# Attention and squared-ReLU layers on one core: norm sums, token scales and the planner's engine choice rewritten

## The chip, the cores and the metric

The kernel runs on one core of one Trainium2 chip. The metric is the device time of one execution in microseconds. Three runs of the kernel before gave 688.0, 686.88 and 683.96 us; their median, 686.88 us, is the time that the change is compared with.

## What is computed

```python
def _attn_ref(q, k, v):                       # 4 batches, 12 heads, 448 tokens, 64 columns
    scores = (1 / sqrt(64)) * q @ k^T         # causal mask, softmax over the last axis
    return attn @ v
def _moe_ref(x, w_in, w_out):                 # x: 1792 tokens x 768; w_in 768 x 2048; w_out 2048 x 768
    r = np.maximum(x @ w_in, 0.0)
    return (r * r) @ w_out
```

The attention output of a batch, with its heads side by side, is the x of the second part. Everything comes in and goes out as float32.

## The kernel before, in words

Matrix products that need more than half precision are made of float16 pieces: a number is split into a high half (the helper `hi`, line 406) and the rest (the helper `lo`, line 419), and three products, high by high, high by rest and rest by high, are summed in PSUM. So that the halves stay in range, tensors are first scaled by powers of two that come from sums of squares (the helper `pow2`, line 436).

Attention works on pairs of heads, 24 pairs in all, six for each batch (`pair`, line 595). Batch 0 is done in float32 (scores on L677, transposes of the probabilities on L706, values on L718), batches 2 and 3 with float16 halves throughout (scores on L663, values on L728), batch 1 with float32 scores and float16 values. VectorE masks the scores and finds the row's extreme (L646), ScalarE takes the exponential (L650). Where values are float16, the normalised probabilities are split into halves in a tile psrc (`halves`, line 580), which a transposing DMA turns (L592). `pair_norm` (line 543) sums the squares of q and k for batches 2 and 3: ScalarE sums along rows (L548), one float32 matmul against a matrix of ones sums over partitions (L552).

The weights are loaded in 24 tiles of w_in and 16 of w_out, narrowed to float32 by integer operations (`narrow`, line 790), measured by Gram matrices on TensorE (L837, L878), and split into halves. In `weights_in` the largest entry of each of four groups is found through a diagonal tile dg (L847), which before is a buffer of the ring of the squares (`n_sq`, line 355), and a matmul with ones (L851).

The second part works on eight sub-blocks of 256 or 128 tokens (`sub_block`, line 928), two for each batch. Each has a head: ScalarE squares x of its six pairs (L938), six matmuls with ones add them over pairs and partitions (L943), three small VectorE operations make a power of two for each token (L950 to L956), three VectorE multiplications rescale x with it (L962), and `tau` (L967) makes the inverse scale on one partition; for each 128 tokens a matmul with one contracted row turns it to lie along partitions (L980), VectorE copies it out (L983) and forms the output factor (L985). Then come 16 blocks of 18 matmuls with w_in (L996), ReLU, square and split of each, and blocks of 6 matmuls with w_out (L1032). The first block of L996 in the program needs the x of all six pairs of batch 0, rescaled, and the first quarter of w_in's halves; the Gram matrices of w_out stand ahead of it in TensorE's queue.

All instructions are collected in a `Plan` (line 68) and put in order by its method `order` (line 149): it runs through a model of the engines, and at each step issues on some engine the ready operation with the smallest due time. Due times come from a table of numbers `PR` (line 21) by phase and kind of operation. Operations that several engines can do (halves, ReLU, copies and so on) carry a cost for each engine plus a bias from the same table; the planner passes over such an operation on an engine if another engine would end it sooner:

```python
if any(max(free.get(o, 0.0), cand[o][i]) + opts[o] + extra[o] < mine - 1e-9
       for o in opts if o != e): continue
```

The engines then execute their queues strictly in this order.

Of the kernel before, what the change touches and what calls it, by code (L numbers as in the profile page):

```python
# [7 lines left out]
F32 = mybir.dt.float32  # L8
# [13 lines left out]
    "bias_dve": 2396, "bias_act": -5582, "bias_pool": 2108, "T0": -417806, "RAMP": 114330, "B1": -987389,  # L22
# [7 lines left out]
    "m_fac": -4151640, "m_ghi": 2453041, "m_glo": -2429258, "m_msq": 1161753, "m_ob": 5245791, "m_relu": -3597239,  # L30
    "m_sig": 2979051, "m_sq": -2069264, "m_tau": 62051, "wi_wl": 127247, "wi_wn": 103676, "wi_wq": 2844441,
    "wo_wl": 2520234, "wo_wn": -2027194, "wo_wq": -1031725, "ws_wn": 2804128, "wt_wn": -555275,
    "a0_P.copy@act": -1188, "a0_P.copy@dve": -2443, "a0_P.nrm@act": -3840, "a0_P.nrm@dve": 4543,
    "a0_P.nrm@pool": 1096, "a0_qk.copy@act": 1118, "a0_qk.copy@dve": -3194, "a0_x.top@act": -2065,
    "a0_x.top@dve": -1734, "m_ghi.hi@act": -3891, "m_ghi.hi@dve": 3617, "m_ghi.hi@pool": -536, "m_glo.lo@dve": 5701,
    "m_glo.lo@pool": 4841, "m_relu.@act": -4348, "m_relu.@dve": -3168, "m_sq.@act": 3841, "m_sq.@dve": -2095,
# [31 lines left out]
class Plan:  # L68
# [80 lines left out]
    def order(self):  # L149
# [32 lines left out]
        while done < n:  # L182
            best = None
            for strict in (True, False):
                for e, c in cand.items():
                    if not c:
                        continue
# [7 lines left out]
                    if best is not None and t >= best[0]:  # L195
                        continue
# [932 lines left out]
```

## Time and profile before

| what | value |
|---|---|
| runs of the kernel | 688.0, 686.88, 683.96 us; median 686.88 us |
| span of the profiled execution, first to last instruction | 683.7 us |
| TensorE matmul busy | 632.0 us, 92% |
| VectorE, ScalarE, GpSimd busy | 349.6, 436.8, 225.2 us |
| mean granted TensorE clock | 0.967 |

The page gives the span of its execution and no device time of that execution beside it; the span lies 3.2 us under the median of the three runs and just under the fastest. A busy share is an average over a first stretch in which weights are prepared and a long one that is mostly matmuls, so the table alone does not say what bounds the time; the rows below are read by stretch. Busy times count overlapping instructions of one engine once, the mean duration of a group does not.

### The profile page before, as it was taken

Reading aid. Unit: us, or ns where it says so; the run is one execution under the profiler, and the core shown is the slowest. Engines: PE = TensorE matmul, PEld = TensorE weight load, DVE = VectorE, ACT = ScalarE, POOL = GpSimd, SP = SyncE. Lnnn points to the kernel's source line nnn. Section 1 sums busy time; section 2 is a strip of 40 time slices with the busy share of each in tenths; the row PEclk is TensorE's granted clock in tenths of the full one; section 3 lists DMA queues with packets and bytes.
Section 4 is the critical chain, followed back from the end, with each engine's and each line's share of the span. In section 5 each row is a group of like instructions: output and inputs, shape, how many; then the busy total and the mean of one; then the engine's idle time right before and its main releaser. Section 6 shows DMA issues by size and latency. Waiting matters only on the chain.

```text
span 683.7 us, 13868 instructions
## 1 busy us (share of the span) xinstructions
PE 632.0 (92%) x5110; PEld 457.6 (67%) x5110; DVE 349.6 (51%) x1027; ACT 436.8 (64%) x1260; POOL 225.2 (33%) x330
## 2 busy tenths in 40 slices
PE   5877779699999999999999999999999999999997
PEld 3554446476667676778675687768867878867864
DVE  3899898989986668788964543520100200200000
ACT  2688887879987997789667975754604434304500
POOL 4333233234521113344234864772302222103200
PEclk9987777989999999999999999999999999999999
DMA  9989886656476889999989936662000000000000
GB/s 263 293 246 283 276 308 220 152 133 121 89 128 132 176 166 177 190 173 177 198 159 184 206 70 102 122 135 43 13 23 13 13 13 1 13 23 12 13 23 24
DMA packets 208676, 87.31 MB, mean 128 GB/s; under 512 B 196064, under 2 KB 203488, under 8 KB 208608
## 3 DMA queue, kind: packets, MB, share of 16 engines
q1 hardware_dynamic: 208608, 86.43, 55.7%
q8 instruction: 40, 0.66, 0.4%
q14 instruction: 28, 0.23, 0.1%
HBM read 45.81 MB, written 5.51 MB: 75 GB/s over the span
## 4 chain that ended last, share of the span: by engine, by line
PE 46%; POOL 3%; DMA 3%; issue 3%; ACT 3%; DVE 2%; SPq 0%; DVEq 0%; POOLq 0%; ACTq 0%
PE bank L996 21%; PE bank L1032 21%; PE bank L728 2%; PE bank L663 1%; POOL psrc L431 1%; DMA raw<-in_k_dram 1%; POOL p L429 1%; DMA pT<-psrc 1%; ACT p L650 1%; DMA kT<-qs 1%; DVE psrc L426 1%; POOL g L421 1%; DVE bank L646 1%; ACT qs L413 0%; PE bank L980 0%
## 5 line engine op out<-in xcount | busy, mean ns | idle before, releaser
L996 PE MATMUL bank<-xt,wi 128*128 128x256 f16 (+1 forms) x2304 | 230.8, 259 | 1.3 <-ACT r L1007 1.2
L1032 PE MATMUL bank<-wo,g 128*128 128x384 f16 x1344 | 230.0, 326 | 0.0
L996 PEld LDWEIGHTS <-wi 128*128 128x128 f16 x2304 | 201.2, 98 | 25.4 <-issue 3.3
L1032 PEld LDWEIGHTS <-g 128*128 128x128 f16 x1344 | 129.4, 98 | 82.8 <-issue 2.9
L421 POOL TENSOR_TENSOR g<-g,g 128x256 f16<-128x256 f32 (+1 forms) x128 | 83.5, 663 | 232.0 <-ACT g L413 139.1
L650 ACT ACTIVATE p<-bank,nm 112x112 f32<-112x112 f32 (+3 forms) x192 | 93.3, 491 | 31.7 <-DVE nm L646 23.6
L1007 ACT ACTIVATE r<-bank 128x256 f32<-128x256 f32 (+1 forms) x128 | 45.4, 355 | 46.5 <-PE bank L996 45.9
L646 DVE CUSTOM_DVE_ANT_0 bank<-bank,mask,sc 112x336 f32<-112x336 f32 (+3 forms) x96 | 47.6, 512 | 51.1 <-PE bank L663 34.3
L1042 ACT ACTIVATE ob<-bank,fac 128x384 f32<-128x384 f32 x28 | 16.1, 578 | 82.4 <-PE bank L1032 82.3
L950 DVE TENSOR_SCALAR u<-bank 128x256 int32<-128x256 int32 (+1 forms) x8 | 3.1, 388 | 107.4 <-PE bank L943 45.7
L1014 ACT ACTIVATE g<-r 128x256 f32<-128x256 f32 (+1 forms) x128 | 48.8, 388 | 13.2 <-POOL g L421 9.6
L413 ACT ACTIVATE psrc<-p,nm 112x112 f16<-112x112 f32 (+2 forms) x106 | 49.7, 530 | 11.2 <-DMA pT<-psrc 8.1
L413 ACT ACTIVATE g<-g 128x256 f16<-128x256 f32 (+1 forms) x128 | 48.1, 389 | 12.9 <-PE bank L1032 11.4
L426 DVE SCALAR_TENSOR_TENSOR psrc<-p,nm,psrc 112x112 f16<-112x112 f32 (+3 forms) x96 | 52.6, 586 | 4.1 <-POOL psrc L415 2.2
L646 DVE CUSTOM_DVE_ANT_0 bank<-bank,mask 112x112 f32<-112x112 f32 (+3 forms) x96 | 41.1, 475 | 17.2 <-PE bank L677 16.9
L677 PE MATMUL bank<-kT,qT 64*112 64x336 f32 (+3 forms) x192 | 40.9, 471 | 6.7 <-ACT p L650 5.8
L706 PE MATMUL bank<-ident,p 112*112 112x112 f32 x120 | 28.9, 382 | 17.9 <-ACT p L566 14.0
L663 PE MATMUL bank<-kT,qT 128*112 128x336 f16 (+3 forms) x192 | 36.0, 286 | 3.4 <-ACT p L650 2.5
L650 ACT ACTIVATION_READ_ACCUMULATOR p<-bank,nm 112x1 f32 x192 | 38.5, 200 | 0.0
L706 PEld LDWEIGHTS bank<-ident,p 112*112 112x112 f32 x120 | 18.1, 187 | 28.8 <-ACT p L566 21.8
L431 POOL TENSOR_TENSOR psrc<-p,psrc 112x112 f16<-112x112 f32 (+3 forms) x48 | 35.0, 729 | 4.0
L728 PE MATMUL bank<-pT,vp 112*64 112x224 f16 (+3 forms) x432 | 31.2, 284 | 4.0 <-DMA pT<-psrc 4.0
(123 smaller groups left out, 747.3 us busy)
## 6 DMA issues: line engine op xcount, KB each, us to landing
raw<-in_moe_w_out_dram SPq DMA_DIRECT2D x8, 768.0 KB, 4.8
xt<-in_moe_w_out_dram SPq DMA_DIRECT2D x8, 768.0 KB, 5.2
xt<-in_moe_w_in_dram SPq DMA_DIRECT2D x11, 512.0 KB, 5.5
out_dram<-ob SPq DMA_DIRECT2D x28, 192.0 KB, 2.0
raw<-in_moe_w_in_dram SPq DMA_DIRECT2D x9, 512.0 KB, 6.5
vn<-in_v_dram SPq DMA_DIRECT2D x18, 224.0 KB, 3.0
raw<-in_v_dram SPq DMA_DIRECT2D x18, 224.0 KB, 3.5
raw<-in_q_dram SPq DMA_DIRECT2D x12, 224.0 KB, 3.4
```

The lines of the kernel that those rows point to most:

```text
L413: nc.scalar.activation(out=o, in_=i, func=ACTF.Copy, scale=s)
L421: return plan.add({"dve": dve_ns(n), "pool": pool2_ns(n)}, lambda e: engines[e].tensor_tensor(out=out(), in0=in_(), in1=top(), op=ALU.subt ...
L426: nc.vector.scalar_tensor_tensor(out=out(), in0=in_(), scalar=scale(), in1=top(), op0=ALU.mult, op1=ALU.subtract)
L646: one("dve", dve_ns(w, 1, 2 if F16S[b] else 1) - 10, lambda e: nc.vector.tensor_tensor_reduce(out=s.ap[0:P, 0:w], in0=s.ap[0:P, 0:w], in1= ...
L650: one("act", act_ns(w, True, 1, True), lambda e: nc.scalar.activation(out=p32[j].ap[:, b0:b0 + c + 1, :].rearrange("p a t -> p (a t)"), in ...
L663: nc.tensor.matmul(out=s.ap[0:P, 0:(c + 1) * P], lhsT=qT.ap[:, j * NCH + c, :], rhs=kT.ap[:, a:a + c + 1, :].rearrange("p a t -> p (a t)") ...
L706: nc.tensor.transpose(t.ap[0:P, (x - a) * P:(x - a + 1) * P], p32[j].ap[:, c * (c + 1) // 2 + kc, :], ident[0:P, 0:P])
L728: nc.tensor.matmul(out=pv.ap[j * D:(j + 1) * D, kc * P:S], lhsT=vp.ap[:, hv, vb:vb + D], rhs=pT[j].ap[0:P, hp * NSL + x:hp * NSL + x + w, ...
L996: nc.tensor.matmul(out=h.ap[:, 0:n], lhsT=wi_hl(ci, hw)[:, ms], rhs=x[:, kd, hx, off:off + n], start=(kd == 0 and hw == 0 and hx == 0), st ...
L1007: nc.scalar.activation(out=r.ap[:, 0:n], in_=h.ap[:, 0:n], func=ACTF.Relu)
L1014: nc.scalar.activation(out=g32.ap[:, 0:n], in_=r.ap[:, 0:n], func=ACTF.Square)
L1032: nc.tensor.matmul(out=o.ap[:, 0:HALF], lhsT=g[:, kf, hg, tt * 128:(tt + 1) * 128], rhs=wo_hl(kf, hw)[:, hh * HALF:(hh + 1) * HALF], start ...
```

## The change

These are its five parts.

1. The six squares of a sub-block lie side by side in one tile `sq`; three VectorE additions in bfloat16 (three pairs, one, one) sum them, and one matmul with ones takes the place of six.
2. The inverse token scale is made on all 128 partitions (it was on one). A VectorE multiplication with the identity matrix that also sums along the row puts it along partitions, in place of the one-row matmul and the copy.
3. The matmul of `pair_norm` reads the upper halves of its float32 sums as bfloat16, in place of float32.
4. The diagonal tile of `weights_in` comes from the ring `vn`, of one buffer, which the loads of v for its norm also use.
5. The planner's choice of an engine is rewritten, and the table `PR` has new numbers throughout. The biases are of another size.

```diff
-    "bias_dve": 2396, "bias_act": -5582, "bias_pool": 2108, ...
+    ... "bias_act": -58819, "bias_dve": 14648, "bias_pool": 43358, ...
@@ order()
+    def elsewhere(self, i, e, t, free, cand):
+        opts, extra = self.ops[i][0], self.bias[i]
+        if len(opts) == 1:
+            return False
+        mine, rank = t + opts[e] + extra[e] - 1e-9, (self.ops[i][3], i)
+        for o in opts:
+            if o == e:
+                continue
+            q = max(free.get(o, 0.0), cand[o][i]) + (opts[o] + extra[o])
+            if q < mine:
+                q += sum(self.ops[j][0][o] for j, r in cand[o].items()
+                         if len(self.ops[j][0]) == 1 and (self.ops[j][3], j) < rank and r < t)
+                if q < mine:
+                    return True
+        return False
...
+                    when = {i: max(r, shared) if locks(i, e) else r for i, r in c.items()}
+                    while when:
+                        t = max(f, min(when.values()))
+                        if best is not None and t >= best[0]:
+                            break
+                        pick = min((self.ops[i][3], i) for i, r in when.items() if r <= t + 1e-9)[1]
+                        if strict and self.elsewhere(pick, e, t, free, cand):
+                            del when[pick]
                             continue
@@ pair_norm
-        one("pe", 310, lambda e: nc.tensor.matmul(
-            out=ps.ap[0:P, 0:2], lhsT=ones_f[0:P, 0:P], rhs=ss.ap[0:P, 0:2].bitcast(F32), start=True, stop=True),
+        one("pe", 60, lambda e: nc.tensor.matmul(
+            out=ps.ap[0:P, 0:2], lhsT=ones_b[0:P, 0:P], rhs=ss.ap[0:P, 0:2].bitcast(BF16)[:, 1::2], start=True, stop=True),
@@ weights_in
-                dg = n_sq([128, SUB], BF16)
+                dg = n_vn([128, VN // NPAIR], F32)
@@ sub_block
-        def norm(e):
-            for pr in range(NPAIR):
-                nc.tensor.matmul(
-                    out=tot.ap[:, 0:n], lhsT=ones_b, rhs=sqs[pr].ap[:, 0:n], start=(pr == 0), stop=(pr == NPAIR - 1))
+        for a, w, z in ((0, 3, 3), (0, 1, 1), (0, 1, 2)):
+            one("dve", dve_ns(w * n, 2), lambda e, a=a, w=w, z=z: nc.vector.tensor_tensor(
+                out=sq[:, a:a + w, 0:n], in0=sq[:, a:a + w, 0:n], in1=sq[:, z:z + w, 0:n], op=ALU.add), ...
+        one("pe", mm_ns(n), lambda e: nc.tensor.matmul(
+            out=tot.ap[:, 0:n], lhsT=ones_b, rhs=sq[:, 0, 0:n], start=True, stop=True), [(sqs, 0)], [tot], due)
...
-                out=u.ap[0:1, 0:n], in0=u.ap[0:1, 0:n], scalar1=142.0, scalar2=E23, op0=ALU.add, op1=ALU.mult)
+                out=u.ap[:, 0:n], in0=u.ap[:, 0:n], scalar1=142.0, scalar2=E23, op0=ALU.add, op1=ALU.mult)
...
-            one("pe", 310, lambda e, tt=tt, tp=tp: nc.tensor.matmul(
-                out=tp, lhsT=u.ap[0:1, tt * 128:(tt + 1) * 128].bitcast(F32), rhs=ones_f[0:1, 0:1],
-                start=True, stop=True), [(u, 2)], [tot], ("m", pos, "tau"))
-            one("dve", 75, lambda e, tp=tp, fc=fc: nc.vector.tensor_copy(out=fc.ap[:, 0:1], in_=tp),
+            one("dve", dve_ns(128), lambda e, tt=tt, fc=fc: nc.vector.tensor_tensor_reduce(
+                out=u.ap[:, tt * 128:(tt + 1) * 128].bitcast(F32), in0=u.ap[:, tt * 128:(tt + 1) * 128].bitcast(F32), in1=ident, scale=1.0,
+                scalar=0.0, op0=ALU.mult, op1=ALU.add, accum_out=fc.ap[:, 0:1]), ...
```

Counted in the two programs, these operations change engine. Of the 144 rests of psrc GpSimd had 48; now VectorE has all of them. Of the 144 high halves of psrc GpSimd had 38; now ScalarE has all of them. Of the high halves of w_in GpSimd had 14 and ScalarE 10; now VectorE has 16 and ScalarE 8. GpSimd gets 12 of the 24 high halves of q and k and 4 more rests of v. VectorE takes 12 of the 24 first copies of the attention output from ScalarE. GpSimd's instructions fall from 335 to 207, VectorE's rise from 1029 to 1136.

Where the order moves is shown at three places. Each listing has the line numbers of its own file (those of the changed one are none to three higher here).

The first place is VectorE's queue from the token scale of the first sub-block to its third rescale (`TENSOR_TENSOR xt<-xt,sg`); `u` and `fac` are the token scale and its output factor. Before:

```order
L968 TENSOR_SCALAR u<-u 1x256
L973 TENSOR_SCALAR u<-u,vst 1x256
L884 TENSOR_REDUCE wst<-bank_149 128x1
L962 TENSOR_TENSOR xt_153<-xt_153,sg 128x4x256
L983 COPY fac<-bank_137 128x1
L904 TENSOR_TENSOR wst<-wst 128x4
L905 TENSOR_REDUCE s_1439<-wst 128x1
L962 TENSOR_TENSOR xt_153<-xt_153,sg 128x4x256
L983 COPY fac<-bank_137 128x1
L962 TENSOR_TENSOR xt_153<-xt_153,sg 128x4x256
```

Now, the last ten rows of it (two rows that read accumulators out are left out):

```order
L963 TENSOR_TENSOR xt_150<-xt_150,sg 128x4x256
L916 TENSOR_SCALAR wst<-wst 128x4
L921 TENSOR_TENSOR wst<-wst 128x1
L922 TENSOR_TENSOR wst<-wst 128x1
L963 TENSOR_TENSOR xt_150<-xt_150,sg 128x4x256
L985 SCALAR_TENSOR_TENSOR fac<-fac,wst 128x1 x2
L649 ISA bank_126,nm<-bank_126,mask 112x336
...
L649 ISA bank_122,nm<-bank_122,mask 112x336
...
L429 SCALAR_TENSOR_TENSOR wo<-wo,wst 128x768
L963 TENSOR_TENSOR xt_150<-xt_150,sg 128x4x256
```

Between the last x of batch 0 (L749) and the third rescale there were 26 instructions, that one and the rescale included; now there are 48.

The second place is SP's queue where the first tile of v for batch 1's norm (`vn<-in_v_dram`) is loaded among the tiles of w_out. Before:

```order
L536 DMA wo<-in_k_dram 112x4x64 [waits DMAHW5_49]
L478 DMA vn<-in_v_dram 128x448 [waits DMAHW6_49]
L785 DMA raw<-in_moe_w_out_dram 128x1536 [waits DMAHW7_49,DVE_49,Activation_49]
L785 DMA raw<-in_moe_w_out_dram 128x1536 [waits DMAHW0_49,DVE_49,Activation_49]
L478 DMA vn<-in_v_dram 128x448 [waits DMAHW6_49,DMAHW1_49,Activation_49]
```

Now:

```order
L788 DMA raw<-in_moe_w_out_dram 128x1536 [waits DMAHW2_49,DMAHW6_49,DVE_49,Activation_49]
L481 DMA vn<-in_v_dram 128x448 [waits DMAHW3_49,PE_49]
L788 DMA xt_151<-in_moe_w_out_dram 128x1536 [waits DMAHW4_49,DMAHW0_49,DVE_49]
L788 DMA xt_151<-in_moe_w_out_dram 128x1536 [waits DMAHW5_49,DMAHW1_49,DVE_49]
L788 DMA raw<-in_moe_w_out_dram 128x1536 [waits DMAHW7_49,DVE_49,Activation_49]
```

The load stood ahead of all tiles of w_out; it now stands behind five of them, waits for TensorE (the matmul that reads the fourth diagonal tile), and has the other eleven behind it.

The third place is VectorE's queue at the head of the last sub-block. Before, from the first of the three small operations:

```order
L950 TENSOR_SCALAR u<-bank_141 128x256
L953 TENSOR_SCALAR u<-u 128x256
L956 TENSOR_SCALAR sg<-u 128x256
L968 TENSOR_SCALAR u<-u 1x256
L973 TENSOR_SCALAR u<-u,vst 1x256
L962 TENSOR_TENSOR xt_154<-xt_154,sg 128x4x256 x3
```

Now, from the additions on:

```order
L943 TENSOR_TENSOR sq<-sq 128x768
L943 TENSOR_TENSOR sq<-sq 128x256 x2
L951 TENSOR_SCALAR u<-bank_138 128x256
L954 TENSOR_SCALAR u<-u 128x256
L957 TENSOR_SCALAR sg<-u 128x256
L969 TENSOR_SCALAR u<-u 128x256
L974 TENSOR_SCALAR u<-u,vst 128x256
L963 TENSOR_TENSOR xt_151<-xt_151,sg 128x4x256
L981 ISA u,fac<-u,ident 128x128
L981 ISA fac 128x1
...
L985 SCALAR_TENSOR_TENSOR fac<-fac,wst 128x1 x2
L963 TENSOR_TENSOR xt_151<-xt_151,sg 128x4x256 x2
```

The output factors have moved in between the first rescale and the other two. On TensorE the matmul of this norm had 4 blocks of L1032 and two one-row matmuls between itself and the next sub-block's first block of L996, and has 5 blocks now.

## Rows read from the trace of the kernel before

**Rows 1.** The page: span, busy time (share) and instructions by engine.
```profile
span 683.7 us, 13868 instructions
PE 632.0 (92%) x5110; PEld 457.6 (67%) x5110; DVE 349.6 (51%) x1027; ACT 436.8 (64%) x1260; POOL 225.2 (33%) x330
```

**Rows 2.** Windows: busy us (xcount) of PE, PEld, DVE, ACT, POOL; clock; DMA.
```profile
20.00:140.00 120.00, 92.01 (x573) 59.22 (x574) 109.79 (x301) 97.18 (x272) 36.45 (x28) 0.82 0.82 250
140.00:680.00 540.00, 528.03 (x4481) 391.71 (x4479) 231.23 (x694) 333.38 (x971) 180.49 (x291) 1.00 0.49 96
```

**Rows 3.** Timeline of PE (start, us): pair 5, and the first block of L996.
```profile
123.55 0.55 PE L626 MATMUL bank<-ident,raw 112*128 112x112 f32 x4
...
125.28 2.11 PE L718 MATMUL bank<-pT,wo 112*64 112x448 f32 x16
...
139.96 2.44 PE L996 MATMUL bank<-xt,wi 128*128 128x256 f16 x18
```

**Rows 4.** PE waits from 140 us on: first and last of seven (total, times, longest).
```profile
PE bank L728 <- DMA pT<-psrc: 4.0, 4, 1.4
...
PE bank L663 <- DMA kT<-kT: 0.5, 1, 0.5
```

**Rows 5.** Chain that ended last (start, us): PE blocks of one line each.
```profile
310.35 1.97 PE bank L996 x18
...
413.16 0.66 PE bank L943 x6
...
416.34 0.31 PE bank L980 x2
...
487.29 0.33 PE bank L943 x6
```

**Rows 6.** PE groups by line: busy us, mean ns, idle before.
```profile
L552 PE MATMUL bank<-ss,ones_f 112*112 112x2 f32 x24 | 3.7, 222 | 1.0 <-ACT junk L548 1.0
```

**Rows 7.** Timeline of DVE around the first rescale (start, us).
```profile
128.83 0.68 DVE L749 SCALAR_TENSOR_TENSOR xt<-bank,vst,xt 128x448 f16<-128x448 f32 x1
...
136.73 0.68 DVE L962 TENSOR_TENSOR xt<-xt,sg 128x1024 f16<-128x1024 f16 x1
137.32 0.75 DVE L426 SCALAR_TENSOR_TENSOR wi<-wi,wst 128x512 f16<-128x512 f32 x1
```

**Rows 8.** DVE groups by line and shape: busy us, mean ns of one.
```profile
L646 DVE DVE_READ_ACCUMULATOR2_ANT nm<- 112x1 f32 x192 | 27.1, 141 | 0.0
...
L426 DVE SCALAR_TENSOR_TENSOR wi<-wi,wst 128x512 f16<-128x512 f32 x24 | 19.9, 830 | 2.0 <-POOL wi L415 2.0
...
L426 DVE SCALAR_TENSOR_TENSOR wo<-wo,wst 128x768 f16<-128x768 f32 x16 | 17.2, 1072 | 1.7 <-ACT wo L413 1.7
...
L962 DVE TENSOR_TENSOR xt<-xt,sg 128x1024 f16<-128x1024 f16 x18 | 11.9, 680 | 0.0
...
L646 DVE CUSTOM_DVE_ANT_0 bank<-bank,mask 112x112 f32<-112x112 f32 x24 | 6.4, 300 | 5.1 <-PE bank L677 5.0
...
L962 DVE TENSOR_TENSOR xt<-xt,sg 128x512 f16<-128x512 f16 x6 | 2.2, 412 | 0.0
```

**Rows 9.** Timeline of SP queue and PE in the front (start, us).
```profile
61.07 0.49 SPq L478 DMA_DIRECT2D vn<-in_v_dram  x1
78.48 2.92 SPq L785 DMA_DIRECT2D xt<-in_moe_w_out_dram  x2
...
82.27 0.80 PE L851 MATMUL bank<-sq,ones_f 128*128 128x128 f32 x2 [0.64 <-DVE sq L847]
```

**Rows 10.** Timeline of DVE and PE before a late sub-block (start, us).
```profile
534.13 0.42 DVE L950 TENSOR_SCALAR u<-bank 128x256 int32<-128x256 int32 x1 [42.82 <-ACT sq L938]
...
535.96 1.88 DVE L962 TENSOR_TENSOR xt<-xt,sg 128x1024 f16<-128x1024 f16 x3
...
538.57 4.65 PE L996 MATMUL bank<-xt,wi 128*128 128x256 f16 x41
```

**Rows 11.** The page: one costly DVE group.
```profile
L426 DVE SCALAR_TENSOR_TENSOR psrc<-p,nm,psrc 112x112 f16<-112x112 f32 (+3 forms) x96 | 52.6, 586 | 4.1 <-POOL psrc L415 2.2
```

More of the change, by code (lines that the diff above doesn't have):

```diff
@@ L190, in order @@
                         f = max(f, dma_free - 1400.0)
-                    if e in ("dve", "pool"):
-                        t = max(f, min(max(r, shared) if locks(i, e) else r for i, r in c.items()))
-                    else:
-                        t = max(f, min(c.values()))
-                    if best is not None and t >= best[0]:
-                        continue
-                    pick = None
-                    for i, r in c.items():
-                        if locks(i, e) and shared > r:
-                            r = shared
-                        if r > t + 1e-9 or (pick is not None and (self.ops[i][3], i) > (self.ops[pick][3], pick)):
-                            continue
-                        opts = self.ops[i][0]
-                        if strict and len(opts) > 1:
-                            extra = self.bias[i]
-                            mine = t + opts[e] + extra[e]
-                            if any(
-                                max(free.get(o, 0.0), cand[o][i]) + opts[o] + extra[o] < mine - 1e-9
-                                for o in opts if o != e
-                            ):
-                                continue
-                        pick = i
-                    if pick is not None:
+                    when = {i: max(r, shared) if locks(i, e) else r for i, r in c.items()}
[6 more added lines that the diff above has]
+                            del when[pick]
+                            continue
                         best = (t, e, pick)
+                        break
                 if best is not None:
@@ L387, in attention_relu2_kernel @@
     psrc = [const.tile([128, 2 * NSL, 128], F16, name=f"psrc{i}") for i in range(2)]
+    sq = const.tile([128, NPAIR, SUB], BF16, name="sq")
+    n_sq = lambda: plan.spot([("sq",)], sq)
     mask = const.tile([P, S], BF16, name="mask")
@@ L511, in v_dn @@
     def v_dn(b):
-        return vst[0:1, 8 * (b % 2) + 7:8 * (b % 2) + 8]
+        return vst[:, 8 * (b % 2) + 7:8 * (b % 2) + 8]
     def raw_of(i):
@@ L933, in sub_block @@
         tot = n_h(b)
-        sqs = []
+        sqs = n_sq()
+        due = ("m", pos, "msq")
         for pr in range(NPAIR):
-            sq = n_sq([128, SUB], BF16)
-            sqs.append(sq)
-            one("act", act_ns(n), lambda e, pr=pr, sq=sq: nc.scalar.activation(
-                out=sq.ap[:, 0:n], in_=x[:, pr, 0, off:off + n], func=ACTF.Square), [xk[pr]], [sq], ("m", pos, "msq"))
-        def norm(e):
-            for pr in range(NPAIR):
-                nc.tensor.matmul(
-                    out=tot.ap[:, 0:n], lhsT=ones_b, rhs=sqs[pr].ap[:, 0:n], start=(pr == 0), stop=(pr == NPAIR - 1))
-        one("pe", NPAIR * mm_ns(n), norm, sqs, [tot], ("m", pos, "msq"))
+            one("act", act_ns(n), lambda e, pr=pr: nc.scalar.activation(
+                out=sq[:, pr, 0:n], in_=x[:, pr, 0, off:off + n], func=ACTF.Square), [xk[pr]], [(sqs, pr)], due)
+        for a, w, z in ((0, 3, 3), (0, 1, 1), (0, 1, 2)):
+            one("dve", dve_ns(w * n, 2), lambda e, a=a, w=w, z=z: nc.vector.tensor_tensor(
+                out=sq[:, a:a + w, 0:n], in0=sq[:, a:a + w, 0:n], in1=sq[:, z:z + w, 0:n], op=ALU.add),
+                [(sqs, i) for i in range(z, z + w)] + [(sqs, i) for i in range(a, a + w)], [(sqs, i) for i in range(a, a + w)], due, port=True)
+        one("pe", mm_ns(n), lambda e: nc.tensor.matmul(
+            out=tot.ap[:, 0:n], lhsT=ones_b, rhs=sq[:, 0, 0:n], start=True, stop=True), [(sqs, 0)], [tot], due)
         u, sg = n_u([128, SUB], I32), n_sg([128, SUB], F16)
```

33 lines of the change are left out of this document (15 added, 18 removed), and 40 rows, old and new, of the table PR.

## The prediction, made before the changed kernel ran

> **What bounds the kernel now.** The page comes first [rows 1]: TensorE is busy for 632.0 of 683.7 us and no other engine comes near it. That share is an average over two regimes, so the windows come next [rows 2]. From 20 to 140 us VectorE is busy for 109.8 of 120 us and TensorE for 92.0, at a mean granted clock of 0.82: the preparation is paced by VectorE. From 140 to 680 us TensorE is busy for 528.0 of 540 us at a granted clock of 1.00, its full level of 2.4 GHz, while VectorE is under half busy. The timeline says why the border is at 140: the first block of L996 starts at 139.96 us [rows 3]. From there to the end two questions count: how much work TensorE has left, and how often it waits. The waits after 140 us are seven kinds of together 10.5 us, the largest 4.0 us for turned probabilities [rows 4]. So the time is the start of the first L996 block, plus TensorE's work behind it, plus some 10 us of waits and a short tail. A change of the time by under 0.5%, 3.4 us, is about what a measurement of this kernel cannot tell from none.
>
> **TensorE's work that goes.** Only what stands behind 140 us counts. A norm of 256 tokens takes 0.66 us for six matmuls, one of 128 tokens 0.33 us [rows 5]; five of six go. After the first sub-block there are five heads of 256 and two of 128 tokens, so 5 x 0.55 + 2 x 0.275 = 3.3 us. The one-row matmul that turns 128 scales takes 0.31 us [rows 5]; 12 of the 14 lie behind 140 us: 3.7 us. The norm sum of q and k is one float32 matmul that shows as two records; 24 records are busy for 3.7 us [rows 6], 0.31 us each of the 12. Its bfloat16 form is not in the trace. It cannot cost more than now, so its gain is bounded below by nothing; a single bfloat16 matmul of 128 columns in the norm took 0.33/6 = 0.055 us, which bounds the gain above by 12 x 0.255 = 3.1 us. I take 0.10 us each, nearer the bfloat16 row, and 2.5 us. Together **9.5 us** go, with ends 7.0 and 10.1.
>
> Here a rule speaks against my reading, and it is a rival below. The rows show blocks of 18 matmuls that take 1.97 us [rows 5] and only 10.5 us of waits in 540; weight loads are busy for 391.7 us of the same stretch, 73% [rows 2]. The Trainium skill's "Perfetto Trace Analysis", section "Identifying the Most-Contended Engine", says that matmul busy share is no good measure of the distance from the roofline and that the share of weight loads is to be read in its place. By the rows the sum has minus 9.5 us; by the rule, read strictly, TensorE has room left and the term may be nothing.
>
> **The first block of L996 comes later.** Between the last x of batch 0, at 128.83 us, and the end of the third rescale, where the next row starts at 137.32, VectorE issued 26 instructions in 8.5 us [rows 7], 0.33 us each. Now there are 48 in the same stretch. At the same pace that is 15.7 us, 7.2 us more. By kinds the 22 extra come to the same: three additions, which the trace does not have; the nearest row is the float16 product of 1024 elements at 0.68 and of 512 at 0.41 us [rows 8], so 0.55, 0.28 and 0.28 us. They could run at the rate of a float32 rest (512 in 0.83), then 2.0 us and not 1.1; nothing lets them cost less than a short instruction each, 0.4 us. Two sums along a row by the identity, nearest the masked minimum of 112 elements with its accumulator read, 0.30 + 0.14 us [rows 8], in place of two copies: some 0.6 us net. One more rest each of w_in (0.83 us), v (taken as that) and w_out (1.07), one high half (at most a rest's 0.83), one more pair of masked chunks (0.88) and eleven short operations at 0.14 or more. That is 7.5 to 8.3 us of durations, of which neighbours overlap by a tenth. Two things give part of it back. TensorE started L996 2.6 us after the third rescale had ended because transposes and scores stood ahead of it; in the new order those can be done while VectorE is still busy, down to a transpose behind a ScalarE copy, and I leave 0.5 us. And the transposes of pair 6, 123.55 to 125.28 us [rows 3], stood ahead of pair 5's values and now stand behind them, so those come 1.7 us earlier. Sum: 7.2 - 2.1 - 1.7 = **3.4 us** later. The ends are 0 (ScalarE has less to do ahead of this point, and VectorE, idle for 10 us between 20 and 140, fills its gaps) and 8 (nothing is given back). VectorE's work up to pair 5's x is the same within 1 us, counted instruction by instruction at the mean durations of its groups, so I put nothing for it.
>
> **A wait that is added.** The first load of v for batch 1 was issued at 61.07 us [rows 9] and now waits for the matmul of the fourth diagonal tile, with eleven tiles of w_out behind it on SP's queue. On VectorE that fourth diagonal tile has moved to where the third one stood, and the third one's matmul ran at 82.27 us [rows 9]. Before, the sixth tile of w_out was issued at 78.48 us. So it comes some 5 us later, and VectorE has at that point two or three tiles in stock, each 1.5 to 3 us of narrowing, and its share of score work in between. I put nothing; without that cover it would be up to 5 us, inside the upper end above.
>
> **The late heads.** In the last three heads nothing else runs on VectorE, so its chain is bare. Before, it took from 534.13 to 537.84 us, and L996 started at 538.57 [rows 10], 0.7 us of room. Now two sums by the identity and two factors stand ahead of the second rescale, 2 x 0.44 + 2 x 0.14 or more, some 1.3 us. The norm ends 0.55 us earlier and TensorE has a block of L1032 more and two one-row pairs fewer to do meanwhile, 0.3 us net. Room of 0.2 us is left; I put 0.2 us of wait for each of three, **0.5 us** in all.
>
> **Engine choice.** 48 rests of psrc of 0.586 us [rows 11] come to VectorE, 28 us, and 12 first copies of x. They fall between 140 and 460 us, where VectorE has room [rows 2]. I put nothing: TensorE's filler, the blocks of L996 and L1032 placed between scores and values of a pair, is the same within 5 us at each pair. Were the cover gone, this is the rival on the slow side.
>
> **The sum.** -9.5 + 3.4 + 0.5 = -5.6 us, against a span of 683.7 us: 678.1 us. The median of the runs lies 3.2 us above that span, and I carry this over: **681.3 us**.
>
> **Rivals.**
> - *The preparation gets no longer.* The port and the queue that GpSimd's splits of w_in took are free, VectorE fills its gaps, and the waits on psrc, a GpSimd chain before, go too. For it: rests of w_in have a mean of 0.83 us where the one at 137.32 took 0.75 [rows 7, 8]. Against: most of those splits come behind 140 us. Time: -9.5 + 0 - 3 (most of the 4.0 us of waits on turned probabilities), 674.4 us.
> - *The start eats the gain.* Nothing is given back, and the SP wait adds: first block 8 us later, 1 us more of waits: 686.4 us, no change to tell.
> - *VectorE becomes what TensorE waits for* (slower). Place: the values of the 18 float16 pairs, which need eight rests of psrc each; VectorE now does all eight, 2.7 more a pair, 1.6 us. It decides if VectorE falls behind TensorE's filler by more than the cover at a pair, so that every one of, say, nine pairs pays its 1.6 us: +14 us on the forecast, 695 us. For it: this was already the largest wait [rows 4]. Against: a rest by GpSimd took two instructions, and VectorE is at 43% in this stretch.
> - *TensorE had room* (the page's rule): the removed work gives nothing back, and the later start stays: 686.9 + 3.4 = 690.3 us. The trace so far speaks against it, since it has almost no waits to fill.
> - *It doesn't do what it says*: the additions could run as slowly as float32 rests. That costs 0.9 us a head and is inside the ranges.
>
> **How the numbers follow.** Forecast 0.44, its own range 677 to 686; no longer preparation 0.20; start eats the gain 0.19; VectorE waits 0.12; TensorE had room 0.05. Faster by over 0.5% is below 683.4 us: 0.36 of the forecast's 0.44, all of the first rival: 0.56. Slower is above 690.3: 0.12, 0.03 of the start that eats the gain, 0.02 of the last: 0.17. The rest, 0.27, is the same. The range that holds 8 in 10 runs from the first rival's 674 to just past the last one's 690; it leaves out the slow rival and a little below: 673 to 690.
>
> **What would show it.** First block of L996 near 143.4 us, not before 140 and not after 148. Behind it, TensorE busy some 9 us less than 528 us over the same blocks, with heads of one matmul in 0.1 us and no one-row matmuls. Waits behind the first block of 9 to 12 us in all; each of the last three heads with under 0.5 us before L996. Additions of 0.55, 0.28 and 0.28 us. Psrc rests on VectorE alone, and waits for turned probabilities no larger than 4.0 us. Wrong it would be if the waits after the first block passed 15 us, or if TensorE's work fell by less than 6 us.

## Result, and the profile after

The changed kernel takes 676.91 us (median of four runs, 675.62 to 678.41), the kernel before on the same chip 687.23 us (a fourth run, 687.57 us, joins the three): ratio 0.9858, 95% interval 0.9825 to 0.9892. It was timed once more beside other kernels (e5): 0.9837, interval 0.9813 to 0.9861. So it is 10 to 11 us faster. The forecast was 5.6 us.

The span of the profiled execution is 675.5 us against 683.7. The page's head and its row of busy times:

```profile
span 675.5 us, 13694 instructions
PE 618.0 (91%) x5030; PEld 448.6 (66%) x5030; DVE 380.3 (56%) x1134; ACT 439.4 (65%) x1275; POOL 153.3 (23%) x202
```

Against [rows 1] TensorE has 14.0 us less to do, GpSimd 71.9 us less and VectorE 30.7 us more. Two stretches in the view of windows, the one ahead of 140 us as in [rows 2], the other from the first block of L996 to the end (columns: stretch, its length, then busy time and instructions of each engine, the granted clock, DMA):

```profile
20.00:140.00 120.00, 85.36 (x563) 57.01 (x562) 113.97 (x319) 96.54 (x265) 33.71 (x27) 0.80 0.80 244
143.08:675.50 532.42, 517.90 (x4405) 383.62 (x4402) 256.09 (x781) 334.11 (x988) 111.36 (x164) 1.00 0.50 98
```

The same stretch of the kernel before:

```profile
139.96:683.70 543.74, 528.07 (x4482) 391.75 (x4479) 231.27 (x694) 333.38 (x971) 180.49 (x291) 1.00 0.49 96
```

Behind the first block the kernel is 11.3 us shorter, and TensorE works 10.2 us less there. Another 0.9 us is the end of the execution: from the issue of the last output to the end of the span it is 3.8 us in the kernel before and 2.8 us now (SP's queue, before and then after):

```profile
679.90 0.33 SPq L1046 DMA_DIRECT2D out_dram<-ob  x1
```

```profile
672.67 0.33 SPq L1046 DMA_DIRECT2D out_dram<-ob  x1
```

This is no effect of the change: in e9, which has the old parts and the old order, the end is as short as now (3.5 us from TensorE's last matmul on, in the kernel before 4.5).

The first block itself comes 3.1 us later (139.96 in [rows 3], now 143.08). The changed kernel's timelines there, VectorE from the last x of batch 0 (L752) to the row behind the third rescale (L963), with one of the new additions, then TensorE:

```profile
126.75 0.68 DVE L752 SCALAR_TENSOR_TENSOR xt<-bank,vst,xt 128x448 f16<-128x448 f32 x1
...
128.63 0.55 DVE L943 TENSOR_TENSOR sq<-sq 128x768 bf16<-128x768 bf16 x1
...
140.08 0.68 DVE L963 TENSOR_TENSOR xt<-xt,sg 128x1024 f16<-128x1024 f16 x1
140.68 0.35 DVE L943 TENSOR_TENSOR sq<-sq 128x384 bf16<-128x384 bf16 x1
```

```profile
140.51 1.84 PE L680 MATMUL bank<-kT,qT 64*112 64x448 f32 x4
142.28 1.01 PE L629 MATMUL bank<-ident,raw 112*128 112x112 f32 x4
143.08 2.76 PE L996 MATMUL bank<-xt,wi 128*128 128x256 f16 x18
145.68 0.55 PE L629 MATMUL bank<-ident,raw 112*128 112x112 f32 x4
```

The waits of TensorE from 143 us to the end (engine, line, releaser: us in all, times, longest) answer to [rows 4]; in sum 10.7 us where there were 10.5:

```profile
PE bank L731 <- DMA pT<-psrc: 3.7, 5, 1.9
PE bank L680 <- ACT p L653: 1.9, 3, 1.2
PE bank L666 <- ACT p L653: 1.9, 6, 0.6
PE bank L555 <- ACT junk L551: 1.3, 1, 1.3
PE bank L996 <- ACT r L1007: 0.9, 1, 0.9
PE bank L731 <- DVE nm L690: 0.7, 1, 0.7
PE bank L666 <- DMA kT<-kT: 0.3, 1, 0.3
```

Two groups of PE in that stretch, the norm sum of q and k and the norm of a head (busy us, mean ns of one):

```profile
L555 PE MATMUL bank<-ss,ones_b 112*112 112x2 bf16 x12 | 2.1, 174 | 1.3 <-ACT junk L551 1.3
L946 PE MATMUL bank<-sq,ones_b 128*128 128x256 bf16 (+1 forms) x7 | 1.8, 257 | 0.0
```

A late head of VectorE, which answers to [rows 10] (start, us):

```profile
531.02 0.42 DVE L951 TENSOR_SCALAR u<-bank 128x256 int32<-128x256 int32 x1 [42.20 <-PE bank L946]
...
533.68 0.28 DVE L981 CUSTOM_DVE_ANT_0 u<-u,ident 128x128 f32<-128x128 f32 x1
533.89 0.08 DVE L981 DVE_READ_ACCUMULATOR2_ANT fac<- 128x1 f32 x1
...
534.37 1.28 DVE L963 TENSOR_TENSOR xt<-xt,sg 128x1024 f16<-128x1024 f16 x2
```

Its last rescale ends at 535.65. TensorE takes up L996 at 535.70, without a wait, straight from the block of L1032 ahead of it.

### The profile page after: what moved, and what is told of

Read it like the earlier page. It is cut to its first block, busy times and chain, and to the rows that moved or that the text cites. A ratio compares the mean times of both kernels' runs of the same rounds, so it can differ in the third digit from the quotient of the medians.

```text
span 675.5 us, 13694 instructions
## 1 busy us (share of the span) xinstructions
PE 618.0 (91%) x5030; PEld 448.6 (66%) x5030; DVE 380.3 (56%) x1134; ACT 439.4 (65%) x1275; POOL 153.3 (23%) x202
## 4 chain that ended last, share of the span: by engine, by line
PE 58%; DMA 14%; DVE 12%; ACT 10%; issue 3%; SPq 2%; POOL 1%; POOLq 0%; ACTq 0%; DVEq 0%
PE bank L1032 25%; PE bank L996 22%; DMA pT<-psrc 4%; PE bank L731 3%; PE bank L666 3%; DVE bank L649 2%; ACT p L653 2%; DVE wi L804 2%; PE bank L680 2%; ACT psrc L416 2%; DMA qT<-qs 1%; ACT p L569 1%; DMA vn<-in_v_dram 1%; DMA raw<-in_moe_w_in_dram 1%; DVE psrc L429 1%
## 5 line engine op out<-in xcount | busy, mean ns | idle before, releaser
L996 PE MATMUL bank<-xt,wi 128*128 128x256 f16 (+1 forms) x2304 | 232.4, 260 | 0.9 <-ACT r L1007 0.9
L1032 PE MATMUL bank<-wo,g 128*128 128x384 f16 x1344 | 230.4, 327 | 0.0
L996 PEld LDWEIGHTS <-wi 128*128 128x128 f16 x2304 | 201.2, 98 | 27.7 <-issue 5.2
L1032 PEld LDWEIGHTS <-g 128*128 128x128 f16 x1344 | 130.4, 98 | 84.4 <-issue 3.8
L429 DVE SCALAR_TENSOR_TENSOR psrc<-p,nm,psrc 112x112 f16<-112x112 f32 (+3 forms) x144 | 70.8, 518 | 11.4 <-ACT psrc L416 10.6
L416 ACT ACTIVATE psrc<-p,nm 112x112 f16<-112x112 f32 (+3 forms) x144 | 65.4, 520 | 6.5 <-DMA pT<-psrc 6.0
L649 DVE CUSTOM_DVE_ANT_0 bank<-bank,mask,sc 112x112 f32<-112x112 f32 (+3 forms) x96 | 48.2, 511 | 15.0 <-PE bank L666 7.8
L416 ACT ACTIVATE g<-g 128x256 f16<-128x256 f32 (+1 forms) x128 | 47.2, 388 | 12.7 <-PE bank L1032 11.4
L680 PE MATMUL bank<-kT,qT 64*112 64x336 f32 (+3 forms) x192 | 39.5, 480 | 10.6 <-ACT p L653 7.9
L649 DVE CUSTOM_DVE_ANT_0 bank<-bank,mask 112x112 f32<-112x112 f32 (+3 forms) x96 | 40.9, 476 | 11.3 <-PE bank L680 8.1
L666 PE MATMUL bank<-kT,qT 128*112 128x112 f16 (+3 forms) x192 | 36.3, 288 | 2.1 <-ACT p L653 1.9
L731 PE MATMUL bank<-pT,vp 112*64 112x448 f16 (+3 forms) x432 | 30.2, 284 | 4.6 <-DMA pT<-psrc 3.7
L731 PEld LDWEIGHTS <-vp 112*64 112x64 f16 x432 | 22.0, 109 | 15.2 <-issue 7.0
L680 PEld LDWEIGHTS bank<-kT,qT 64*112 64x112 f32 x192 | 16.4, 188 | 20.9 <-ACT p L653 14.1
## 6 DMA issues: line engine op xcount, KB each, us to landing
out_dram<-ob SPq DMA_DIRECT2D x28, 192.0 KB, 1.9
```

The lines of the kernel that those rows point to most:

```text
L416: nc.scalar.activation(out=o, in_=i, func=ACTF.Copy, scale=s)
L429: nc.vector.scalar_tensor_tensor(out=out(), in0=in_(), scalar=scale(), in1=top(), op0=ALU.mult, op1=ALU.subtract)
L649: one("dve", dve_ns(w, 1, 2 if F16S[b] else 1) - 10, lambda e: nc.vector.tensor_tensor_reduce(out=s.ap[0:P, 0:w], in0=s.ap[0:P, 0:w], in1= ...
L666: nc.tensor.matmul(out=s.ap[0:P, 0:(c + 1) * P], lhsT=qT.ap[:, j * NCH + c, :], rhs=kT.ap[:, a:a + c + 1, :].rearrange("p a t -> p (a t)") ...
L680: nc.tensor.matmul(out=ss[j].ap[0:P, 0:(c + 1) * P], lhsT=f32t(q32)[r, c * P:(c + 1) * P], rhs=f32t(k32)[r, 0:(c + 1) * P], start=True, st ...
L731: nc.tensor.matmul(out=pv.ap[j * D:(j + 1) * D, kc * P:S], lhsT=vp.ap[:, hv, vb:vb + D], rhs=pT[j].ap[0:P, hp * NSL + x:hp * NSL + x + w, ...
```

## The experiments

Lines have the numbers of each kernel's own file. "Parts" are the parts 1 to 3 of the change; part 4 stays as the kernel has it whose order is kept, and no run tests it alone. Most kernels keep the finished order of one of the two kernels: the planner still sees that kernel's operations and costs, so every queue has the same sequence, and only what an operation issues is another. The table splits each profiled execution at two points that all of them have: the first block of L996, and the first block of the sixth sub-block (each sub-block has 16; blocks are counted from 0 below), behind which there is no attention any more (its last values start at 467 us before, at 462 us after). Ratios are medians to the kernel before on the same chip; the other columns are us from the traces.

| run | operations, order | ratio (95%) | first block | to the sixth sub-block | rest | PE busy, waits behind the first block |
|---|---|---|---|---|---|---|
| before | old, old | 1 | 139.96 | 350.8 | 192.9 | 528.1, 10.5 |
| e1 | new parts, old order | 0.9972 (0.9951 to 0.9993) | 138.01 | 354.1 | 189.2 | 522.5, 16.7 |
| e6 | the same, additions earlier | 0.9993 (0.9968 to 1.0018) | 137.50 | 353.4 | 189.8 | 522.4, 16.4 |
| e9 | old parts, old order, psrc choice | 1.0025 (1.0001 to 1.0050) | 138.96 | 353.6 | 192.0 | 529.2, 12.7 |
| e10 | new parts, old order, psrc choice | 1.0021 (0.9992 to 1.0049) | 138.81 | 355.1 | 190.0 | 524.3, 16.7 |
| e11 | new parts, planned by the old table | 1.0369 (1.0324 to 1.0413) | 144.69 | 378.5 | 189.2 | 534.7, 28.5 |
| e12 | old parts, planned by the new table | 1.0065 (1.0036 to 1.0094) | 137.86 | 361.0 | 191.0 | 534.2, 14.1 |
| e2 | old parts, new order | 1.0040 (1.0021 to 1.0060) | 146.55 | 350.8 | 190.4 | 527.1, 10.1 |
| e3 | six matmuls, new order | 0.9889 (0.9864 to 0.9914) | 145.06 | 343.3 | 188.3 | 519.5, 8.0 |
| e4 | one-row matmuls, new order | 0.9975 (0.9954 to 0.9997) | 146.01 | 346.4 | 189.3 | 522.5, 9.3 |
| after | new, new | 0.9858 (0.9825 to 0.9892) | 143.08 | 345.2 | 187.2 | 517.9, 10.7 |
| e5 | new, new, again | 0.9837 (0.9813 to 0.9861) | 143.27 | 343.6 | 187.2 | 516.6, 10.1 |
| e7 | new, rests of batch 3 on GpSimd | 1.0138 (1.0115 to 1.0161) | 144.68 | 361.4 | 187.2 | 520.9, 23.7 |
| e8 | new, 16 matmuls added | 0.9811 (0.9785 to 0.9838) | 144.21 | 340.0 | 187.2 | 516.5, 6.6 |

**What of a trace repeats (e5).** No edit.

> The changed kernel itself, as the yardstick for the runs beside it and to see what of a trace repeats. Expected: ratio 0.983 to 0.989, about 675 to 678 us; first block of L996 at 143.1 us within 2 us, and the granted clock at its lower level for the stretch just ahead of that block, as in the first trace.

Measured: the second trace has every block within 0.6 us of the first up to block 28, then comes 1.0 to 1.5 us ahead: the first had one dip of the granted clock near 260 us (0.87 from 256 to 262), this one has none (1.00). The first block comes at 143.27 us, with the granted clock at 0.68 from 126 to 140, both as expected. Executions of the changed kernel spread over 3 us, of the kernel before over 7 us (682.5 to 690.2). So the ratios decide, and a trace says where.

**The parts on the old order (e1, e6).** Part 1, in the operation of the norm (e6 issues the additions behind the sixth square instead):

```diff
-            for pr in range(NPAIR):
-                nc.tensor.matmul(out=tot.ap[:, 0:n], lhsT=ones_b, rhs=sqs[pr].ap[:, 0:n], ...
+            for a, w, z in ((0, 3, 3), (0, 1, 1), (0, 1, 2)):
+                nc.vector.tensor_tensor(out=sq6[:, a:a + w, ...], in0=sq6[:, a:a + w, ...], in1=sq6[:, z:z + w, ...], op=ALU.add)
+            nc.tensor.matmul(out=tot.ap[:, 0:n], lhsT=ones_b, rhs=sq6[:, 0, ...], start=True, stop=True)
...
-            one("pe", 310, lambda e, tt=tt, tp=tp: nc.tensor.matmul(...
+            one("pe", 310, lambda e: None, ...
```

> The kernel before, its order and engine choice kept, with only the additions and the one norm matmul, the sums by the identity and the bfloat16 norm sum of q and k put in place. Theory (TensorE's work behind the first block of L996 sets the end; the work taken away comes back in full): TensorE's busy time behind the first block falls by 9.4 us (3.3 norms, 4.5 one-row matmuls, 1.6 norm sums of q and k, by the two traces shown), first block 0 to 2 us later than 139.96 for the additions and sums by the identity on VectorE, waits as before: 677 to 680 us, ratio 0.986 to 0.990. Rival A (the new order and engine choice gave the gain): 684 us or more, ratio above 0.995. Rival B (TensorE had room, the removed matmuls give nothing): 687 us or more, the waits grow by what the matmuls gave.

> As e1 (the parts on the kernel before's own order), but with the three additions issued behind the sixth square and not at the place of the norm matmul, so that TensorE need not wait for them there; e1 had 3.8 us of waits on the additions behind the first block. Theory C (e1 fell short of its 9.4 us mainly by these waits): they go, 679 to 681 us, ratio 0.991 to 0.994. Theory D (what the matmuls free in the stretch with attention is taken up by waits for ScalarE and VectorE, whatever the additions do; only the late heads return it): 682 to 684 us, ratio 0.996 to 0.999, and the waits of the scores on the exponential stay near 7 us.

Measured: 0.9972 and 0.9993. Of e1's three, rival A fits; of e6's theories D, the gain even a little smaller. The window of e1 from its first block, then two of its waits there:

```profile
138.01:681.30 543.29, 522.51 (x4411) 386.44 (x4408) 245.07 (x729) 334.35 (x972) 182.85 (x291) 1.00 0.48 96
```

```profile
PE bank L671 <- ACT p L658: 7.6, 12, 1.2
PE bank L954 <- DVE sq L951: 3.8, 3, 1.7
```

TensorE works 5.6 us less than before, and the stretch is just 0.5 us shorter: the waits took the rest. The 5.6 us are less than the 9.4 expected, as some work that stayed took longer: the blocks of L996 up to the sixth sub-block are busy for 151.99 us where they were for 150.31, and the granted clock is 0.74 from 138 to 145 us, around the first block. Up to the sixth sub-block e1's trace is even 3.3 us longer than that of the kernel before. In e6 the additions are waited for 1.3 us in place of 3.8, and the scores wait more instead. From 250 to 350 us, scores for the exponential, in the kernel before and in e6:

```profile
PE bank L663 <- ACT p L650: 2.0, 3, 1.2
```

```profile
PE bank L671 <- ACT p L658: 6.2, 8, 1.3
```

The exponential in turn waits for VectorE's mask, 5.1 us before and 8.5 us in e6:

```profile
ACT p L650 <- DVE nm L646: 5.1, 8, 1.9
```

```profile
ACT p L658 <- DVE nm L654: 8.5, 10, 2.0
```

So in the stretch with attention the removed matmuls had been work done while TensorE would have waited, and it now waits. Behind it, where nothing but L996, L1032 and heads run, the parts return 2.2 to 2.8 us (192.0 in e9, which has the old parts and the usual end, to 189.8 and 189.2).

**The old parts on the new order (e2), and one part each (e3, e4).** The opposite edits in the changed kernel; in e3 the additions issue nothing, in e4 the operation of the identity sum issues the one-row matmul and the copy, e2 has both and the float32 norm sum.

```diff
-            one("dve", dve_ns(128), lambda e, tt=tt, fc=fc: nc.vector.tensor_tensor_reduce(...
+            one("dve", dve_ns(128), turned, ...
```

> The changed kernel, its order and engine choice kept, with the six norm matmuls, the one-row matmuls with copies and the float32 norm sum put back. Theory: 9.4 us of TensorE's work come back behind the first block, the first block starts 1 to 2 us earlier than 143.1 for the VectorE work that goes: 684 to 686 us, ratio 0.995 to 0.999. Rival A (order and engine choice gave the gain): 676 to 680 us, ratio under 0.990. Rival B (TensorE had room): 675 to 678 us, with waits smaller by the work that came back.

> The changed kernel with the three additions left out and six norm matmuls again, nothing else. Theory: TensorE's busy time behind the first block grows by 3.3 us, the first block starts 0 to 1 us earlier: 678.5 to 680.5 us, ratio 0.987 to 0.991. Rival (the additions cost on VectorE what the matmuls gave on TensorE, or TensorE had room): 675 to 677.5 us, ratio under 0.986.

> The changed kernel with the inverse token scale on one partition, one-row matmuls and VectorE copies again, nothing else. Theory: 12 one-row matmuls behind the first block cost TensorE 0.31 to 0.38 us each, 3.7 to 4.5 us, first block 0 to 0.6 us earlier: 680 to 681.5 us, ratio 0.989 to 0.992. Rival (the late heads of the changed kernel wait for VectorE by the sums, so that the old way costs less than it takes): 677 to 679 us.

Measured: e2 1.0040, e3 0.9889, e4 0.9975. Only e3 lies in the range of its theory; e2 and e4 are slower than any of their theories had them. On the new order the parts are worth 1.8 to 2.0%, over 12 us; e3 and e4 show where. From the first block of the seventh sub-block to that of the eighth, with one head of 256 tokens between, the changed kernel takes 48.12 us, e3 48.67, e4 49.17, e2 49.71: the five matmuls cost 0.55 us a head, as forecast, the two one-row matmuls 1.05 us. Of these, 0.25 us is a wait for VectorE's copy, which the kernel before has not: its order has a block of L1032 between the two. From e4:

```profile
538.59 0.38 PE L984 MATMUL bank<-ones_f,u 1*128 1x1 f32 x2 [0.25 <-DVE fac L987]
```

The start was not as expected: it comes later with the old parts, by 2.0 us in e3, 2.9 in e4, 3.5 in e2. In e3 the six matmuls are on the way to the rescale, at a time of lower clock (granted 0.50 from 131 to 136 us): 1.49 us where the changed kernel has one of 0.30. In e4 VectorE waits, in its timeline:

```profile
136.77 0.15 DVE L987 COPY fac<-bank 128x1 f32<-128x1 f32 x1
139.58 0.16 DVE L987 COPY fac<-bank 128x1 f32<-128x1 f32 x1 [2.66 <-PE bank L984]
...
139.78 0.68 DVE L963 TENSOR_TENSOR xt<-xt,sg 128x1024 f16<-128x1024 f16 x1
```

and the reason stands in TensorE's queue:

```profile
137.57 1.47 PE L680 MATMUL bank<-kT,qT 64*112 64x336 f32 x4 [1.57 <-ACT p L653]
138.96 0.58 PE L984 MATMUL bank<-ones_f,u 1*128 1x1 f32 x2
```

The second one-row matmul stands behind scores that wait for ScalarE; VectorE's copy waits for it, and all three rescales wait behind the copy. The identity sum stays on VectorE and breaks this loop. That the matmul stands there is the frozen order's doing; a planner that knew of it could have put it elsewhere (e12).

**Who makes psrc (e7, e9, e10).** The kernels keep the order and override the engine, first e7 in the changed kernel, then e9 in the kernel before and e10 in e6:

```diff
+            if n >= 36:
+                fn = plan.ops[k][1]
+                plan.ops[k] = plan.ops[k][:1] + (lambda e, fn=fn: fn("pool"),) + plan.ops[k][2:]
...
+            for z, to in ((k - 1, "act"), (k, "dve")):
+                ...
```

> The changed kernel with the 48 rests of psrc of batch 3 on GpSimd again, where the kernel before had them; order and all else kept. Theory (VectorE has room there, it does not matter who makes the rests): within 1 us of the changed kernel, ratio 0.984 to 0.988. Rival (the move of the rests to VectorE gave the gain beyond the forecast, by a shorter chain to the turned probabilities): 2 to 5 us slower than the changed kernel, with more wait of L731 on pT between 330 and 430 us.

> The kernel before, its order kept, with one thing of the new engine choice: all 144 high halves of psrc on ScalarE and all 144 rests on VectorE (before, GpSimd had 38 and 48). Theory F (the halves of psrc on GpSimd are what keeps attention behind TensorE from 250 to 440 us: rests on VectorE beside GpSimd's halves take 0.64 us there and 0.52 in the changed kernel): 680 to 684 us, ratio 0.990 to 0.996, rests on VectorE under 0.55 us, waits of scores on the exponential no more than 2.5 us. Rival G (the order, the sequence itself, must fit the engines' times; the choice alone moves work into queues that were laid out for another): no change or slower, ratio 0.998 to 1.02, with waits of TensorE grown.

> e6 with the engine choice of e9: the additions, the one norm matmul, the sums by the identity, the bfloat16 norm sum, and psrc's halves on ScalarE and VectorE alone, all in the order of the kernel before. Theory F: the matmuls that go are returned once psrc is off GpSimd: 676 to 680 us, ratio 0.985 to 0.990, waits behind the first block near 10 us and not 16. Rival G: 684 us or more, ratio above 0.996, waits of 15 us or more: what the parts free is returned only by an order that is planned for them.

Measured: e7 1.0138, 20.7 us behind e5 and far over what the rival had. Most of the loss, 16 us beside e5's trace, lies between 347 and 482 us, and not in the rival's waits for turned probabilities (5.9 us in all, 5.3 in e5). TensorE's waits from 350 to 440 us, what the exponential waits for from 330 to 450 us, and what GpSimd needs there for one rest (two instructions, by line):

```profile
PE bank L669 <- ACT p L656: 6.8, 5, 2.7
PE bank L555 <- ACT junk L551: 2.3, 2, 1.4
```

```profile
ACT p L656 <- POOL psrc L434: 6.4, 3, 3.1
```

```profile
L434 POOL TENSOR_TENSOR psrc<-p,psrc 112x112 f16<-112x112 f32 (+3 forms) x36 | 26.4, 733 | 3.0
L432 POOL TENSOR_SCALAR p<-p,nm 112x112 f32<-112x112 f32 (+3 forms) x36 | 19.2, 533 | 18.4 <-ACT psrc L416 18.4
```

That is 1.27 us, where VectorE needs 0.52: the scores wait for the exponential, and it waits for GpSimd's rests, a wait that the changed kernel does not have. The kernel before has the very same rests on GpSimd, in an order that was planned with them there, and its L663 waits for the exponential for 2.5 us in all where e7's L669 waits 11.0. The other way round, e9 and e10 give VectorE the rests and ScalarE the high halves in the old order. The rests do get faster, 638 ns in the kernel before and 518 in e9 (both from 250 to 350 us):

```profile
L426 DVE SCALAR_TENSOR_TENSOR psrc<-p,nm,psrc 112x336 f16<-112x336 f32 (+3 forms) x51 | 30.7, 638 | 2.5 <-POOL psrc L415 2.2
```

```profile
L426 DVE SCALAR_TENSOR_TENSOR psrc<-p,nm,psrc 112x336 f16<-112x336 f32 (+3 forms) x50 | 24.7, 518 | 8.1 <-ACT psrc L413 8.0
```

but scores wait more for ScalarE, and the time is 0.2% longer. Theory F falls, G stands: in the old sequence the parts bring 0.1 to 0.3%, the choice for psrc and both together nothing. The other changes of engine were not tried there.

**The planner left free (e11, e12).** e11 is the changed kernel with the old table and the old rule, e12 the kernel before with the new ones; so the planner knows the operations in both. Table and rule go together in both, so what either does alone is not shown.

> The changed kernel's operations and their costs, planned with the table and the engine choice rule of the kernel before, so that the planner knows the additions and the sums by the identity and can place them. Theory H (the parts bring their 9 us wherever the planner knows of them; e1 and e6 only placed them badly): 676 to 681 us, ratio 0.985 to 0.992. Rival G (they need the new table and rule too): 683 us or more, ratio above 0.995.

> The operations of the kernel before, with their costs, planned with the new table and the new engine choice rule (e2 kept the changed kernel's finished order; here the planner knows the six matmuls and the one-row matmuls and can place them). Theory P (the gain is the plan's, and the parts are incidental): 676 to 680 us, ratio under 0.991. Theory Q (gain only where parts and plan fit, as e1, e2, e6, e9 and e10 have it): 685 us or more, ratio above 0.998; as the table was made for other operations it may be far more, as e11 was with 711.

Measured: 1.0369 and 1.0065. Theories H and P fall. In e11 TensorE runs out of work twice and loses the clock (windows; the clock is the third number from the end):

```profile
140.00:180.00 40.00, 29.55 (x179) 19.36 (x178) 38.22 (x78) 21.86 (x64) 17.80 (x17) 0.80 0.53 121
...
295.00:316.00 21.00, 13.26 (x79) 9.82 (x79) 19.22 (x75) 14.23 (x42) 4.35 (x9) 0.51 0.98 196
```

e12 has its first block at 137.86 us, 5.2 us ahead of the changed kernel, and is 14 us slower: an early first block is no gain by itself.

**Filling TensorE's idle time (e8).**

```diff
+    def warm(k):
+        for _ in range(k):
+            nc.tensor.matmul(out=bank[0][:, 0:128], lhsT=ones_f, rhs=ones_f, start=True, stop=True)
```

> The changed kernel with 16 float32 matmuls of ones by ones added on TensorE, in its idle times between 127 and 139 us (5 behind the second transposes of pair 6, 4 behind the norm of the first sub-block, 6 behind the second scores of pair 6, 1 behind the first transposes of pair 7); nothing reads what they make. The changed kernel had the lower clock from 130.7 to 144.4 us. Theory (what ends the preparation is partly TensorE's own work at the lower clock: about 5 us of scores, transposes and the first block there would take half): the granted clock is at its full level ahead of the first block, and the kernel is 1.5 to 2.5 us faster than the changed one, ratio 0.982 to 0.984. Rival (VectorE's chain of the head sets the start alone): first block at the same time, gain under 1 us; or slower by the added work, up to 2 us.

Measured: 673.09 us beside 675.47 for e5, the fastest of all, though the two intervals overlap. The difference, 2.4 us, is of the size that the theory had, but does not come by its way. The clock was up from 126 to 140 us and then down just where it was wanted. The changed kernel, then e8:

```profile
126.00:140.00 14.00, 6.54 (x35) 3.71 (x34) 13.86 (x49) 10.20 (x32) 2.29 (x2) 0.67 0.74 176
140.00:147.00 7.00, 6.97 (x42) 4.44 (x41) 5.51 (x19) 5.50 (x15) 0.00 (x0) 0.69 0.56 129
```

```profile
126.00:140.00 14.00, 9.18 (x79) 7.24 (x77) 13.81 (x47) 10.86 (x31) 2.30 (x2) 0.99 0.79 188
140.00:147.00 7.00, 6.36 (x26) 3.91 (x27) 6.12 (x20) 5.55 (x15) 0.00 (x0) 0.51 0.53 133
```

Its first block is 1.1 us later than the changed kernel's, and still 0.6 us later than e5's at block 28. What it gains, it gains between blocks 28 and 56, where the waits are smaller (6.6 us in all). Why, is open.

## Why the prediction was right, and where it was not

The time lies 4.4 us under the forecast and inside the range. By the steps:

- *TensorE's work that goes, 9.5 us.* Right in sum: busy time behind the first block fell by 10.2 us (11.5 in e5). The norm term is exact (0.55 us a head, e3). The one-row term was too small: in the old order the way from the seventh to the eighth sub-block falls from 50.52 to 49.10 us with the new parts (e1), which leaves, less the norm's 0.55, 0.87 us for two and not 0.62. The norm sum of q and k was too large a gain: the bfloat16 matmul takes 0.174 us where I took 0.10, so 1.6 us and not 2.5.
- *That it all comes back.* Right for this order, wrong as an argument. I took TensorE's small waits as proof that removed work is removed time. In the old order it was not (e1, e6): there the outcome of my least likely rival, "TensorE had room", came in the whole stretch with attention, by waits for ScalarE and VectorE. The Trainium skill, "Perfetto Trace Analysis", section "Identifying the Most-Contended Engine", warns against matmul busy share as a measure of how close a kernel is to the roofline; here it did not show either what removed work brings, being 97% behind the first block before and after. The share of weight loads, one of the two measures that the page puts in its place, does not tell the two orders apart here either: 72% of that stretch before and after, 71% in e1.
- *The first block, 3.4 us later.* Measured 3.1 us (3.3 in e5), but by luck: two terms of the sum are off by 1.8 and 1.9 us and cancel. VectorE's 48 instructions from the last x, at 126.75 us, to the row behind the third rescale, at 140.68, took 13.9 us, 0.29 us each where I took 0.33, so 5.4 us more than before and not 7.2. And of the 2.6 us between the rescale and the first block I gave 2.1 back, but 2.4 us are still there: TensorE had scores and transposes to do ahead of L996, and four transposes took it 1.01 us, at a granted clock of 0.69 from 140 to 147 us, where they take 0.55 at 145.68. I left the clock out. The third term held: the last x came 2.1 us earlier where I had 1.7.
- *The late heads, 0.5 us.* No wait came, as the 0.2 us of room that I had reckoned already said; the term had no ground. VectorE's bare chain, 531.02 to 535.65 us, ends just as TensorE is through with its blocks of L1032.
- *Engine choice, nothing.* This step failed. I asked only if VectorE had room for the rests and took the order of the rest as neutral. In the changed order the rests of batch 3 on VectorE are worth 20 us (e7); in the old one all rests there, with the high halves on ScalarE, cost 0.2% (e9). So there is no value of the choice for psrc by itself, nor of the parts (0 to 2 us in the old order, 12 in the new), nor of the order (2.7 us slower with the old parts, e2; 4.5 with the planner free, e12). The gain is of the combination.
- *The v wait, nothing,* and *waits behind the first block, 9 to 12 us*: as said. The sixth tile of w_out was issued at 78.07 us and not 5 us after the 78.48 of before; VectorE waited once for a tile of w_out there, 2.1 us. The waits behind the first block are 10.7 us; turned probabilities 3.7 us, though 5.3 in the second trace (e5), over the 4.0 that I had as their most.
- *From span to median, 3.2 us.* The rows now show the device time of an execution to lie 1.7 us over its span (677.23 and 675.5). The execution profiled before thus took, by this estimate, some 685.4 us, 1.5 us under the median that I had, and I put these 1.5 us on the changed kernel as well. This and 2.3 us more behind the first block (11.3 against 9.5 less 0.5; 0.9 of it the end of the execution, which the change did not shorten) make most of the 4.4 us.

What it is in the new sequence that covers the attention chain, beyond psrc, was not separated: the 12 first copies, the high halves of q and k on GpSimd and the places of the blocks differ all at once. Why e1's trace loses 3.3 us in that stretch, and not just gains nothing, is open too.

## What to carry to other kernels

Small waits on the busiest engine do not prove that its removed work comes back: in a sequence that was fitted to its operations the removed work may have been what covered a chain of other engines. Test it by changing what the operations issue while the order stands, in both orders; four kernels (old and new operations in old and new order) say more than any one. A table of order numbers belongs to the operations that it was made with; with others it can lose more than twice what they gain (e11: 26 us).

## What the runs showed of the hardware

A block of 18 matmuls of L996 took 4.00 us at the lower clock (granted 0.50), 1.97 at the full one ([rows 5]):

```profile
137.86 4.00 PE L998 MATMUL bank<-xt,wi 128*128 128x256 f16 x18
```

That is the first block of e12. Sums in bfloat16 on VectorE took 0.55 us for 768 elements in most heads; the sum along a row by the identity took 0.28 us and 0.08 us for the accumulator's read, less than the 0.30 and 0.14 that I had from the masked minimum. Rests of psrc ran at 638 ns while GpSimd made high halves and at 518 ns when ScalarE did; by shape, those of 112 elements at 572 and 333 ns, those of 448 at 680 and 681, so the largest lost nothing. And the sequence behind the sixth sub-block repeats to 0.01 us: 187.2 us in after, e5, e7 and e8, although the stretches ahead of it differ by 22 us.
